# Weight conversions moved across the passes of a fast matrix product, decay rows from a scan, and a weight buffer placed elsewhere

## The chip, the cores and the metric

One core of a Trainium2 chip runs the whole kernel. The metric is the device time of one execution in microseconds (us); lower is better. The engines are named TensorE (PE; its weight loads PEld), VectorE (DVE), ScalarE (ACT), GpSimd (POOL) and SyncE (SP), whose queue issues every transfer of this kernel.

## What is computed

Three stages in a row, all in float32 precision (each float32 operand of a product is split into a high and a low part, and three products are summed).

```python
scores = scale * q @ k.T + (cum_i - cum_j)        # cum = cumsum(log(clip(f, 1e-4, 1)))
attn   = softmax(causal(scores)) ;  x = attn @ v  # 4 batches x 8 heads, 576 x 64
h = relu(x @ w_in) ** 2 ;  x = h @ w_out          # 2304 tokens, 512 -> 2048 -> 512
g = sigmoid(x @ w_gate) * (x @ w_val)             # 512 -> 1536
out = g @ w_out2                                  # 1536 -> 512
```

The weights arrive as float64. Each block of 128 x 512 is turned into float32 and split by a chain called a conversion: `conv_a` is an Abs on ScalarE (L128), `conv_b` four bit operations on VectorE (L143, L144, L147, L150; the last writes the single buffer `wf`), `conv_c` the high part on ScalarE (L164) and the low part on GpSimd (L165).

## The kernel before

**Setup and attention** (L186 to L526). `setup` (L233) loads f and takes its clipped logarithm on 32 partitions (one per head). The running sum over 576 positions is made on TensorE: the logarithms are transposed (L270), split into two parts, and multiplied with a triangle of ones (L284); the two halves of the result are copied and split (L289, L290) and written to the DRAM buffer `cum_d` (L293). `load` (L217) brings q, k and v of a pair of heads in three transfers each (L224 twice, L228). The 16 pairs of heads run through a software pipeline, whose order is a written list (`ORDER`, L499), step name and lag: TQ and TK transpose q and k (L298), qh, ql, kh, kl split them, S01 to S4 make the scores (L334, L407), R the row minima on VectorE, X the exponentials, M the normalisation on GpSimd (L422), G the transposes of the attention rows (L433), PV the product with v (L467). The decay enters the scores as one more product, with `cr`, two rows (high and low) for each of the two heads. `cr` is loaded from `cum_d` at the step kh of a pair (L384), two small transfers, and S01 of the pair reads it first.

**First up stage** (L570 on): x @ w_in, relu and square, spilled to DRAM.

**First down stage** (L705 to L766): h @ w_out, done by a scheme with seven block products in place of eight. `steps` (L605) has seven passes k_ = 0 to 6, each of 3 column groups (jj) times 4 steps (w); a step has 12 matmuls (L757). Two steps ahead, `d_split` (L613) splits a block of activations into the pair buffer `gg`, on ScalarE (L617) and VectorE (L618). VectorE also splits the weight sums `ao` (L603) in the last third of a pass and adds the finished sums (L704, L710). The order inside the stage is the program's own (`manual_schedule`). In pass 5, the block at L738 adds the conversions of the first gate and the first value block of the third stage, one phase in a step, for 12 steps.

**Second up and down stages** (L770 on). The third stage's weights are converted through `conv_q`; the scheduler may place these instructions earlier, among those of the down stage, where their buffers let it. Even blocks go to the pool `wi0`; odd ones to the pool `wi2` (L770), which before lies at the right end of SBUF, where the down stage's first weights lay.

Of the kernel before, what the change touches and what calls it, by code (L numbers as in the profile page):

```python
# [40 lines left out]
def kernel(  # L41
# [163 lines left out]
    ones_f = pts[:, 0:S]  # L205
# [2 lines left out]
    ones_u = qk[1]["kh"][:, 0:S]
    fT = qk[1]["kl"][:, 0:2 * NC * BH].rearrange("p (t c) -> p t c", t=2)
# [22 lines left out]

    def setup():  # L233
        nc.sync.dma_start(out=f_sb, in_=f.rearrange("b h s -> (b h) s"))
        for p in range(2):
# [2 lines left out]
        nc.gpsimd.memset(ones_f, 1.0)
        nc.gpsimd.affine_select(
            out=ones_f, in_=ones_f, pattern=[[1, S]], compare_op=ALU.is_ge, fill=0.0, base=0, channel_multiplier=-1  # L240
        )
        for nm_ in "qkv":
            for t in nat[nm_]:
                nc.gpsimd.memset(t[64:128, NF, :, :], 0.0)
        nc.vector.tensor_copy(ones_u, ones_f)
        for d in qk:
            for nm_ in ("cr", "eh", "el"):
                nc.gpsimd.memset(d[nm_].bitcast(F32), 0.0)
        for t in pt_t:
            nc.gpsimd.memset(t[:, 2 * POFF[NF] + S:2 * POFF[NF] + PC], 0.0)  # L250
# [20 lines left out]
        for n, w0, w1 in ((128, 0, NF * BH), (REM, NF * BH, NC * BH)):  # L271
            nc.scalar.activation(out=fT[0:n, 0, w0:w1], in_=fps[0:n, w0:w1], func=AF.Copy)
            nc.vector.tensor_tensor(
                out=fT[0:n, 1, w0:w1], in0=fps[0:n, w0:w1], in1=fT.bitcast(F32)[0:n, 0, w0:w1], op=ALU.subtract
            )
        for a, e in ((0, 256), (256, S)):
            cps = ps2()
            for c in range(NC):
                n = 128 if c < NF else REM
                s = max(a, c * 128)  # L280
                if s >= e:
                    continue
                for t in range(2):
                    nc.tensor.matmul(  # L284
                        cps[0:BH, s - a:e - a], lhsT=fT[0:n, t, c * BH:(c + 1) * BH],
                        rhs=ones_u[0:n, s - c * 128:e - c * 128],
                        start=(c == 0 and t == 0), stop=(t == 1 and c == min(NF, (e - 1) // 128)),
                    )
            nc.scalar.activation(out=cum_s[:, a:e], in_=cps[0:BH, 0:e - a], func=AF.Copy)  # L289
            nc.vector.tensor_tensor(  # L290
                out=cum_s[:, S + a:S + e], in0=cps[0:BH, 0:e - a], in1=cum_s.bitcast(F32)[:, a:e], op=ALU.subtract
            )
        nc.sync.dma_start(out=cum_d, in_=cum_s.bitcast(F32).rearrange("p (t s) -> p t s", t=2))  # L293
# [575 lines left out]
```

## Time and profile before

| | us |
|---|---|
| median of 3 runs | 1057.94 |
| the three runs | 1058.1, 1057.94, 1053.87 |
| the profiled execution | 1053.46 |
| its span, first to last instruction | 1051.6 |
| TensorE busy in the span | 1014.5 |
| VectorE / ScalarE / GpSimd busy | 561.8 / 484.6 / 254.6 |

The profile is of one execution. The attention takes the first 205 us or so, the first up stage runs to about 411, the first down stage from 411.3 to 600.2, the second up stage to about 900, and the last product to the end. TensorE's busy time counts pipelined matmuls and overlaps a little, so that where it shows a full window the engine had always something running.

### The profile page before, as it was taken

What the parts mean: (1) busy time and instruction counts of PE and PEld (TensorE: products, weight loads), DVE (VectorE), ACT (ScalarE), POOL (GpSimd) and SP (SyncE); (2) the same over time, 40 slices, a digit from 0 to 9 for tenths busy, and PEclk for the clock granted to TensorE, in tenths of its full rate; (3) what the DMA queues carried; (4) which work ended last, traced back from release to release, by engine and by line L of the source; (5) the groups of instructions that cost most, each with busy time, mean ns of one, the idle gap of its engine ahead of it and who ended that gap; (6) DMA issues with size and microseconds to landing.
All of it is one profiled execution on the core that took longest, in us unless ns stands there. A gap on an engine that the chain in (4) does not pass through costs nothing.

```text
span 1051.6 us, 16437 instructions
## 1 busy us (share of the span) xinstructions
PE 1014.5 (96%) x5915; PEld 899.2 (86%) x5915; DVE 561.8 (53%) x1131; ACT 484.6 (46%) x992; POOL 254.6 (24%) x330
## 2 busy tenths in 40 slices
PE   4999999899999999999997899999999999999998
PEld 3788788699999999999997788888888888888886
DVE  2878778555666664687689823434333421233222
ACT  3788778556666665564565422222222221222222
POOL 3766666510000121061035411111111110000000
PEclk8999999999999999999999999999999999999999
DMA  5333333057787779766665423333333311244343
GB/s 122 70 85 88 70 81 87 21 183 243 246 259 255 247 242 303 198 187 195 189 190 165 163 76 123 128 123 118 120 125 112 106 65 48 80 134 140 102 119 110
DMA packets 139217, 150.35 MB, mean 143 GB/s; under 512 B 65024, under 2 KB 110080, under 8 KB 139136
## 3 DMA queue, kind: packets, MB, share of 16 engines
q1 hardware_dynamic: 139136, 149.31, 47.4%
q8 instruction: 46, 0.75, 0.3%
q14 instruction: 35, 0.29, 0.1%
HBM read 97.21 MB, written 52.05 MB: 142 GB/s over the span
## 4 chain that ended last, share of the span: by engine, by line
PE 89%; DVE 3%; issue 3%; SPq 2%; DMA 1%; ACT 0%; POOL 0%; DVEq 0%; POOLq 0%; ACTq 0%
PE ps L549 29%; PE ps L573 18%; PE ps L812 14%; PE ps L757 13%; PE pa L334 4%; PE pa L467 4%; PE pa L433 3%; PE pa L298 2%; PE pa L407 2%; DVE gg L618 1%; SPq L224 1%; DMA cr<-cum_d 1%; SPq L228 1%; PE pa L439 1%; DVE wtmp L144 1%
## 5 line engine op out<-in xcount | busy, mean ns | idle before, releaser
L549 PE MATMUL ps<-xT,hl 128*128 128x512 f32 (+1 forms) x1440 | 300.1, 371 | 0.0
L549 PEld LDWEIGHTS ps<-xT,hl 128*128 128x128 f32 x1440 | 250.8, 188 | 49.3 <-DVE yt L710 0.3
L573 PE MATMUL ps<-xT,hl 128*128 128x384 f32 x1152 | 200.6, 335 | 1.9 <-ACT hl L164 1.1
L573 PEld LDWEIGHTS ps<-xT,hl 128*128 128x128 f32 x1152 | 199.7, 188 | 2.6 <-ACT hl L164 1.5
L757 PE MATMUL ps<-gg,ao 128*128 128x384 f32 x1008 | 178.3, 336 | 10.9 <-DVE gg L618 10.7
L757 PEld LDWEIGHTS ps<-gg,ao 128*128 128x128 f32 x1008 | 174.3, 188 | 14.8 <-DVE gg L618 14.0
L165 POOL TENSOR_TENSOR hl<-wf,hl 128x512 fp32r<-128x512 f32 x52 | 68.9, 1325 | 382.3 <-ACT hl L164 380.9
L812 PE MATMUL ps<-hl,gg 128*128 128x512 f32 x648 | 147.1, 389 | 0.0
L812 PEld LDWEIGHTS ps<-hl,gg 128*128 128x128 f32 x648 | 121.5, 188 | 25.2
L422 POOL TENSOR_TENSOR pt<-pt,sm 128x128 f32<-128x128 f32 (+2 forms) x144 | 105.8, 767 | 54.2 <-DVE sm L417 53.9
L618 DVE TENSOR_TENSOR gg<-gl,gg 128x768 fp32r<-128x768 f32 x84 | 90.5, 1081 | 40.7 <-ACT gg L617 40.5
L617 ACT ACTIVATE gg<-gl 128x768 fp32r<-128x768 f32 x84 | 71.0, 846 | 66.5 <-PE ps L757 48.0
L791 DVE TENSOR_TENSOR gg<-gi,gg 128x512 fp32r<-128x512 f32 (+1 forms) x60 | 38.4, 640 | 101.7 <-ACT gg L790 101.7
L834 DVE TENSOR_TENSOR r<-ps,r 128x512 f32<-128x512 f32 (+1 forms) x60 | 38.2, 636 | 101.8 <-PE ps L549 97.1
L641 DVE TENSOR_TENSOR gt<-gt 128x384 f32<-128x384 f32 x96 | 52.0, 584 | 70.9 <-ACT gt L675 70.9
L832 ACT ACTIVATE r<-ps 128x512 f32<-128x512 f32 (+1 forms) x60 | 32.8, 547 | 119.1 <-PE ps L549 119.1
L320 ACT ACTIVATE pt<-pt,nm 128x128 f32<-128x128 f32 (+1 forms) x144 | 82.5, 583 | 10.1 <-DVE nm L312 10.0
L790 ACT ACTIVATE gg<-gi 128x512 fp32r<-128x512 f32 (+1 forms) x60 | 35.4, 589 | 105.3 <-PE ps L812 102.3
L150 DVE SCALAR_TENSOR_TENSOR wf<-wraw,wtmp 128x512 int32<-128x512 int32 x68 | 47.8, 702 | 51.4 <-POOL hl L165 49.4
L674 ACT ACTIVATE gt<-ps 128x384 f32<-128x384 f32 x96 | 46.8, 488 | 59.4 <-PE ps L573 53.2
L312 DVE CUSTOM_DVE_ANT_0 pt<-pa,maskc 128x128 f32<-128x128 f32 (+2 forms) x144 | 67.1, 513 | 11.6 <-PE pa L334 10.8
L128 ACT ACTIVATE wtmp<-wraw 128x512 f32<-128x512 f32 x68 | 44.7, 658 | 61.7 <-DMA wraw<-in_moe_w_out_dram 41.3
(99 smaller groups left out, 1009.3 us busy)
## 6 DMA issues: line engine op xcount, KB each, us to landing
g<-gt SPq DMA_DIRECT2D x168, 192.0 KB
gl<-g SPq DMA_DIRECT2D x84, 384.0 KB
wraw<-in_moe_w_out_dram SPq DMA_DIRECT2D x28, 512.0 KB
g<-r SPq DMA_DIRECT2D x48, 256.0 KB
gi<-g SPq DMA_DIRECT2D x48, 256.0 KB
wraw<-in_moe_w_in_dram SPq DMA_DIRECT2D x16, 512.0 KB
wraw<-in_moe_w_gate_dram SPq DMA_DIRECT2D x12, 512.0 KB
wraw<-in_moe_w_val_dram SPq DMA_DIRECT2D x12, 512.0 KB
```

What stands on the lines that cost most here:

```text
L150: lambda: nc.vector.scalar_tensor_tensor(out=t.bitcast(I32), in0=lo, scalar=29, in1=xi, op0=ALU.logical_shift_right, op1=ALU.bitwise_or),
L165: nc.gpsimd.tensor_tensor(out=hl[:, 1, :], in0=t, in1=hl.bitcast(F32)[:, 0, :], op=ALU.subtract)
L312: nc.vector.tensor_tensor_reduce(out=o, in0=s, in1=mask, scale=1.0, scalar=3.0e38, op0=ALU.add, op1=ALU.min, accum_out=nm_t[p % 2][:, c:c ...
L320: nc.scalar.activation(out=x, in_=x, func=AF.Exp, bias=nm_t[p % 2][:, c:c + 1], scale=-1.0, accum_out=sm_t[p % 2][:, c:c + 1])
L422: nc.gpsimd.tensor_tensor(out=x, in0=x, in1=sm_t[p % 2][:, c:c + 1].to_broadcast([128, e - a]), op=ALU.mult)
L549: nc.tensor.matmul(h[:, 0:n], lhsT=a, rhs=x[:, b_, :], start=(c == 0 and i == 0), stop=(c == KD - 1 and i == 2))
L573: nc.tensor.matmul(h, lhsT=a, rhs=xT[c][:, b_, t0:t0 + BT], start=(c == 0 and i == 0), stop=(c == KD - 1 and i == 2))
L617: nc.scalar.activation(out=s[:, 0], in_=t, func=AF.Copy)
L618: nc.vector.tensor_tensor(out=s[:, 1], in0=t, in1=s.bitcast(F32)[:, 0], op=ALU.subtract)
L641: nc.vector.tensor_tensor(out=t, in0=a, in1=b_, op=ALU.subtract)
L757: nc.tensor.matmul(o, lhsT=ws[:, a, u, cs], rhs=s[:, b_, u, :], start=(k_ in (0, 2, 5) and w == u == x == 0), stop=(w == NW - 1 and u == 1 ...
L812: nc.tensor.matmul(o, lhsT=gg[:, a, cs], rhs=w[:, b_, :], start=(k_ == 0 and x == 0), stop=(last and x == 2))
```

## The change

1. **Setup.** The sum over positions is one VectorE instruction, `tensor_tensor_scan`, along the free axis of the 32 partitions; its high part is copied by ScalarE and its low part made by VectorE. The products, transposes and copies of L267 to L292 go, and so do the triangle of ones on GpSimd and its copy on VectorE. `cr` of the first two pairs comes straight from SBUF (`cr_load`), in the queue behind q and k of pair 1; `cum_d` is still written, and later pairs read it in a step of their own, CR, first in the list of an iteration. Memsets that only later steps need move to `setup_late`, the loads of v into the iterations, and setup is now inside the written order.
2. **Conversions.** The gate and value blocks are converted over passes 1 to 4, one phase in each column group (at w = 1), where before all was in pass 5.
3. **Odd weight buffers.** The pool `wi2` is placed from the left (low) end of SBUF, next to `wi0`.

```diff
+    def cr_load(p, source):
+        d = qk[p % 2]
+        for t in range(2):
+            nc.sync.dma_start(out=d["cr"].bitcast(F32)[t:t + 65:64, :], in_=source[2 * p:2 * p + 2, t, :])
...
+        nc.scalar.activation(out=f_sb, in_=f_sb, func=AF.Ln)
+        nc.scalar.activation(out=sm_t[0][0:BH, 0:1], in_=f_sb[:, 0:1], func=AF.Exp)
+        nc.vector.tensor_tensor_scan(out=cum_f, data0=f_sb, data1=f_sb, initial=0.0, op0=ALU.add, op1=ALU.min)
+        nc.scalar.activation(out=cum_s[:, 0:S], in_=cum_f, func=AF.Copy)
+        nc.vector.tensor_tensor(
+            out=cum_s[:, S:2 * S], in0=cum_f, in1=cum_s.bitcast(F32)[:, 0:S], op=ALU.subtract
+        )
...
+        load(1, "q")
+        cr_load(0, cum_v)
+        load(1, "k")
+        cr_load(1, cum_v)
+        nc.sync.dma_start(out=cum_d, in_=cum_v)
...
-        fps = ps2()
-        for c in range(NC):
-            n = 128 if c < NF else REM
-            nc.tensor.transpose(fps[0:n, c * BH:(c + 1) * BH], f_sb[:, c * 128:c * 128 + n], ident[0:BH, 0:BH])
...
+    def CR(p):
+        if p > 1:
+            cr_load(p, cum_d)
...
-        for h in range(2):
-            nc.sync.dma_start(out=d["cr"].bitcast(F32)[64 * h:64 * h + 2, :], in_=cum_d[2 * p + h, :, :])
...
-        S01+0 M2a+1 X4+1 M1b+1 E3+2 R0a+0 R1b+0 X3b+1 PV+2 R0b+0 R1a+0 TQ-1 M2b+1 X3a+1
+        CR-1 S01+0 M2a+1 X4+1 M1b+1 E3+2 R0a+0 R1b+0 X3b+1 PV+2 R0b+0 R1a+0 TQ-1 M2b+1 X3a+1
...
-        if k_ == 5:
-            n = NX + (3 * jj + w) // 5
-            ph = (4 * jj + w) % 6
-            n = NX + (4 * jj + w) // 6
+        if 1 <= k_ <= 4 and w == 1:
+            n, ph = divmod(3 * (k_ - 1) + jj, 6)
+            n += NX
             if ph == 0:
-                load_units(NX + 2)
                 conv_a(*units[n])
-            elif ph == 1:
                 cv[n] = conv_b(*units[n], todo=todo)
-            if todo:
-                todo.pop(0)()
+            if ph < 5:
+                if todo:
+                    todo.pop(0)()
             if ph == 5:
                 conv_c(*units[n], wi_p[0], "wi", cv.pop(n))
...
-    wi_p[1] = ctx.enter_context(tc.tile_pool(name="wi2", bufs=2, side="right", reuse_waits="tile"))
+    wi_p[1] = ctx.enter_context(tc.tile_pool(name="wi2", bufs=2, reuse_waits="tile"))
```

How the instructions moved is shown at two places. The first is SyncE's queue in the setup (cr_159 is the decay tile of pair 0, qn, kn and vn are q, k and v as loaded). Before, behind the loads of k of pair 1 and of v of pair 0:

```order
L224 DMA vn_153<-in_v_dram 128x4x64 x2
L228 DMA vn_153<-in_v_dram 64x2x64
L293 DMA cum_d<-pts 32x1152
L224 DMA vn_154<-in_v_dram 128x4x64 x2
L228 DMA vn_154<-in_v_dram 64x2x64
L224 DMA qn_148<-in_q_dram 128x4x64 x2
L228 DMA qn_148<-in_q_dram 64x2x64
L224 DMA kn_150<-in_k_dram 128x4x64 x2
L228 DMA kn_150<-in_k_dram 64x2x64
L384 DMA cr_159<-cum_d 2x576 x2
```

And now, from q of pair 1 on:

```order
L222 DMA qn_149<-in_q_dram 128x4x64 x2
L226 DMA qn_149<-in_q_dram 64x2x64
L234 DMA cr_159<-pts 2x576 x2
L222 DMA kn_151<-in_k_dram 128x4x64 x2
L226 DMA kn_151<-in_k_dram 64x2x64
L234 DMA cr_164<-pts 2x576 x2
L263 DMA cum_d<-pts 32x1152
```

The decay rows of pair 0 stand in front of k of pair 1. Six loads of three transfers each that stood ahead of them (k of pair 1, v of pairs 0 to 2, q and k of pair 2) are behind them.

The second place is VectorE in pass 5 of the first down stage, from the end of its second column group on (gg is the activation block that the next matmuls read, wtmp and wf belong to conversions, yt is a finished sum). Before:

```order
L710 TENSOR_TENSOR yt<-ps_2684,pu_4892 128x384
L710 TENSOR_TENSOR yt<-ps_2685,pu_4892 128x384
L618 TENSOR_TENSOR gg<-gl,gg 128x768
L603 TENSOR_TENSOR ao<-as,ao 128x512
L144 TENSOR_SCALAR wtmp<-wtmp 128x512
L143 TENSOR_SCALAR wtmp<-wtmp 128x512
L618 TENSOR_TENSOR gg<-gl,gg 128x768
L603 TENSOR_TENSOR ao<-as,ao 128x512
L147 SCALAR_TENSOR_TENSOR wtmp<-wraw,wtmp 128x512
L618 TENSOR_TENSOR gg<-gl,gg 128x768
L603 TENSOR_TENSOR ao<-as,ao 128x512
L150 SCALAR_TENSOR_TENSOR wf<-wraw,wtmp 128x512
```

And now, the same steps:

```order
L702 TENSOR_TENSOR yt<-ps_2657,pu_4865 128x384
L702 TENSOR_TENSOR yt<-ps_2658,pu_4865 128x384
L610 TENSOR_TENSOR gg<-gl,gg 128x768
L595 TENSOR_TENSOR ao<-as,ao 128x512
L610 TENSOR_TENSOR gg<-gl,gg 128x768
L595 TENSOR_TENSOR ao<-as,ao 128x512
L610 TENSOR_TENSOR gg<-gl,gg 128x768
L595 TENSOR_TENSOR ao<-as,ao 128x512
```

The conversions between the splits are gone here and in pass 6. The scheduler's own choices moved with the written ones: the blocks beyond the first gate and value are also begun earlier, in passes 3 to 5, and then stop. In the first column group of pass 3 four conversion instructions now stand in one step:

```order
L610 TENSOR_TENSOR gg<-gl,gg 128x768 x2
L143 TENSOR_SCALAR wtmp<-wtmp 128x512 x2
L144 TENSOR_SCALAR wtmp<-wtmp 128x512
L147 SCALAR_TENSOR_TENSOR wtmp<-wraw,wtmp 128x512
L610 TENSOR_TENSOR gg<-gl,gg 128x768 x2
L696 TENSOR_TENSOR pu_4865<-ps_2657,pu_4863 128x384
```

Three of the four belong to a block that the scheduler chose, not the written order. On VectorE the passes now hold this many conversion instructions: pass 1 three, pass 2 one, pass 3 six, pass 4 five, pass 5 three, pass 6 none; two more stand between the last finished sum and the first product of gate and value. Before, passes 1 to 4 held none and passes 5 and 6 all.

## Rows read from the trace of the kernel before

**Rows 1.** The page's chain that ended last, shares of the span by engine.

```profile
PE 89%; DVE 3%; issue 3%; SPq 2%; DMA 1%; ACT 0%; POOL 0%; DVEq 0%; POOLq 0%; ACTq 0%
```

**Rows 2.** Waits of TensorE, whole span: us in total, times, longest.

```profile
PE ps L757 <- DVE gg L618: 10.7, 10, 2.5
PE pa L334 <- DMA cr<-cum_d: 10.1, 5, 7.8
```

**Rows 3.** Timeline of the setup: start us, us, engine, line, [idle before <-releaser].

```profile
2.84 0.49 DVE L264 TENSOR_SCALAR pts<-pts 32x576 f32<-32x576 f32 x1 [2.84 <-DMA pts<-in_f_dram]
...
3.36 0.68 ACT L265 ACTIVATE pts<-pts 32x576 f32<-32x576 f32 x1 [1.27 <-DVE pts L264]
...
4.06 1.28 ACT L266 ACT_TABLE_LOAD   x1
...
4.20 0.61 SPq L228 DMA_DIRECT2D kn<-in_k_dram  x1
...
6.04 0.61 SPq L228 DMA_DIRECT2D qn<-in_q_dram  x1
...
9.30 1.23 PE L298 MATMUL pa<-ident,kn 128*128 128x128 f32 x5
...
9.54 0.65 ACT L355 ACTIVATE qh<-pa 128x576 fp32r<-128x576 f32 x1 [0.19 <-PE pa L298]
...
11.26 0.76 DVE L388 TENSOR_TENSOR kl<-pa,kh 128x576 fp32r<-128x576 f32 x1 [0.27 <-ACT kh L382]
...
18.43 0.74 SPq L384 DMA_DIRECT2D cr<-cum_d  x2
...
20.29 0.70 PE L334 MATMUL pa<-cr,one_l 64*128 64x128 f32 x2 [7.78 <-DMA cr<-cum_d]
```

**Rows 4.** Windows: stretch, its length, busy us (x) by engine, granted clock, DMA.

```profile
18.00:20.00 2.00, 0.00 (x0) 0.00 (x0) 0.00 (x0) 0.00 (x0) 0.00 (x0) 0.50 0.62 139
```

**Rows 5.** Timeline of the second pair's start, GpSimd and TensorE.

```profile
27.82 3.47 POOL L422 TENSOR_TENSOR pt<-pt,sm 128x128 f32<-128x128 f32 x6 [2.57 <-DVE sm L417]
...
28.52 0.72 PE L334 MATMUL pa<-cr,one_l 64*128 64x128 f32 x2 [0.86 <-DMA cr<-cum_d]
```

**Rows 6.** Waits of TensorE from 30 to 216 us.

```profile
PE pa L334 <- DMA cr<-cum_d: 1.4, 3, 0.9
```

**Rows 7.** Windows of passes 3 and 4, then of pass 5 and pass 6: PE, PEld, DVE, ACT, POOL.

```profile
487.80:513.20 25.40, 25.40 (x148) 25.40 (x147) 17.64 (x24) 12.71 (x17) 0.00 (x0) 1.00 0.69 192
513.20:538.60 25.40, 25.40 (x149) 25.40 (x148) 17.96 (x24) 13.93 (x21) 5.25 (x4) 1.00 0.66 186
538.60:564.00 25.40, 23.17 (x133) 22.63 (x131) 23.82 (x25) 16.69 (x25) 15.53 (x10) 1.00 0.64 187
564.00:600.00 36.00, 28.63 (x153) 26.36 (x154) 33.99 (x41) 16.32 (x25) 15.44 (x11) 1.00 0.53 168
```

**Rows 8.** Groups on VectorE, 411 to 600 us, the four conversion operations: busy us, mean ns.

```profile
L143 DVE TENSOR_SCALAR wtmp<-wtmp 128x512 f32<-128x512 f32 x7 | 7.9, 1122 | 0.0
L147 DVE SCALAR_TENSOR_TENSOR wtmp<-wraw,wtmp 128x512 int32<-128x512 int32 x7 | 6.2, 888 | 0.2
...
L144 DVE TENSOR_SCALAR wtmp<-wtmp 128x512 int32<-128x512 int32 x7 | 5.6, 796 | 0.1
L150 DVE SCALAR_TENSOR_TENSOR wf<-wraw,wtmp 128x512 int32<-128x512 int32 x5 | 4.2, 847 | 0.0
```

**Rows 9.** Timeline in pass 5: two conversions, GpSimd beside them, and TensorE's wait.

```profile
560.70 0.41 DVE L144 TENSOR_SCALAR wtmp<-wtmp 128x512 int32<-128x512 int32 x1
560.86 1.40 POOL L589 TENSOR_TENSOR as<-wf 128x512 f32<-128x512 f32 x1 [0.63 <-DVE ao L603]
561.04 1.50 DVE L143 TENSOR_SCALAR wtmp<-wtmp 128x512 f32<-128x512 f32 x1
...
564.26 2.36 PE L757 MATMUL ps<-gg,ao 128*128 128x384 f32 x12 [2.50 <-DVE gg L618]
```

**Rows 10.** The page's group of the second up stage's matmuls: busy, mean, idle before.

```profile
L549 PE MATMUL ps<-xT,hl 128*128 128x512 f32 (+1 forms) x1440 | 300.1, 371 | 0.0
```

More of the change, by code (lines that the diff above doesn't have):

```diff
@@ L204 @@
     one_l = ap_.tile([128, 256], F32R, name="one_l")
[L205 removed]
+    cum_f = pts[0:BH, 0:S]
     f_sb = pts[0:BH, S:2 * S]
     cum_s = pts[0:BH, 2 * S:4 * S].bitcast(F32R)
[L208 to L209 removed]
     ring = [0]
@@ L231, in load @@
             )
+    def cr_load(p, source):
+        d = qk[p % 2]
+        for t in range(2):
+            nc.sync.dma_start(out=d["cr"].bitcast(F32)[t:t + 65:64, :], in_=source[2 * p:2 * p + 2, t, :])
     def setup():
         nc.sync.dma_start(out=f_sb, in_=f.rearrange("b h s -> (b h) s"))
-        for p in range(2):
-            load(p, "qk")
         make_identity(nc, ident)
[L238 to L242, printed above, removed]
+        for nm_ in "qk":
             for t in nat[nm_]:
                 nc.gpsimd.memset(t[64:128, NF, :, :], 0.0)
-        nc.vector.tensor_copy(ones_u, ones_f)
+        load(0, "qk")
+        nc.vector.tensor_scalar(f_sb, f_sb, 1.0e-4, 1.0, op0=ALU.max, op1=ALU.min)
+        nc.scalar.activation(out=f_sb, in_=f_sb, func=AF.Ln)
[5 more added lines that the diff above has]
+        )
         for d in qk:
[L247 to L250, printed above, removed]
+            nc.gpsimd.memset(d["cr"].bitcast(F32), 0.0)
+        for nm_ in ("eh", "el"):
+            nc.gpsimd.memset(qk[0][nm_].bitcast(F32), 0.0)
         nc.gpsimd.memset(one_l.bitcast(F32), 0.0)
@@ L263, in setup, with setup_late @@
             )
-        nc.vector.tensor_scalar(f_sb, f_sb, 1.0e-4, 1.0, op0=ALU.max, op1=ALU.min)
-        nc.scalar.activation(out=f_sb, in_=f_sb, func=AF.Ln)
-        nc.scalar.activation(out=sm_t[0][0:BH, 0:1], in_=f_sb[:, 0:1], func=AF.Exp)
-        fps = ps2()
-        for c in range(NC):
-            n = 128 if c < NF else REM
-            nc.tensor.transpose(fps[0:n, c * BH:(c + 1) * BH], f_sb[:, c * 128:c * 128 + n], ident[0:BH, 0:BH])
[L271 to L293, printed above, removed]
+    def setup_late():
+        for nm_ in ("eh", "el"):
+            nc.gpsimd.memset(qk[1][nm_].bitcast(F32), 0.0)
+        for t in nat["v"]:
+            nc.gpsimd.memset(t[64:128, NF, :, :], 0.0)
+        for t in pt_t:
+            nc.gpsimd.memset(t[:, 2 * POFF[NF] + S:2 * POFF[NF] + PC], 0.0)
+    def CR(p):
+        if p > 1:
+            cr_load(p, cum_d)
     def transpose_in(t):
@@ L486 @@
     STEP = {
-        "TQ": TQ, "qh": qh, "ql": ql, "EH": EH, "EL": EL, "TK": TK, "kh": kh, "kl": kl,
+        "CR": CR, "TQ": TQ, "qh": qh, "ql": ql, "EH": EH, "EL": EL, "TK": TK, "kh": kh, "kl": kl,
         "S01": S01, "S2": S2, "S3": S3, "S4": S4, "PV": PV,
@@ L507 @@
         conv_q.append(("in", m, wi_p[0], "wi"))
-    setup()
     order = tc.manual_schedule()
     order.__enter__()
-    for p in range(3):
-        load(p, "v")
+    setup()
     steps = [(w[:-2], int(w[-2:])) for w in ORDER]
@@ L516 @@
     for it in range(min(lags), NP + max(lags)):
+        if it == 0:
+            setup_late()
+        if 0 <= it < 3:
+            load(it, "v")
         for nm_, lag in steps:
```

3 lines of the change are left out of this document (added).

## Prediction

> **What bounds the kernel.** I read the chain of waits first: TensorE holds 89% of it [rows 1], so a microsecond off another engine counts only where TensorE stands still for it. TensorE's waits come next. Two kinds cost about 10 us each: the first down stage's matmuls wait for the split activations of VectorE, and the attention's scores wait for the decay rows `cr` [rows 2]. The change touches both.
>
> The setup's timeline shows the second. The scores of pair 0 have nothing left but the product with `cr`, and start it at 20.29 after 7.78 us of standing still [rows 3]. The small transfer was issued only at 18.43, because it stands in SyncE's queue behind loads that nobody waits for yet. [...]
>
> The windows show the first. In passes 3 and 4 TensorE is busy for all of 25.40 us, and VectorE for 17.64 and 17.96. In pass 5 VectorE rises to 23.82, in the rest to 33.99 of 36.00, and TensorE falls to 23.17 and 28.63 [rows 7]. TensorE's idle time there is 2.23 + 7.37 = 9.6 us, nearly all of the 10.7. What was added is conversions: the four groups sum to 7.9 + 6.2 + 5.6 + 4.2 = 23.9 us [rows 8]. Without them VectorE would need 23.82 + 33.99 - 23.9 = 33.9 us of 61.4.
>
> **Term A, the setup: 10.4 us.** Now the path to the first use of `cr` is this. The clip ends at 2.84 + 0.49 = 3.33, the logarithm at 3.36 + 0.68 = 4.04 [rows 3]; both stay. The scan follows on VectorE. No row shows a scan: the nearest are the clip, 0.49 over the same 32 x 576, and the two-input subtract `kl`, 0.76 over 576 columns [rows 3]; I take 0.76 and allow double. Beside it ScalarE loads a table until 4.06 + 1.28 = 5.34 [rows 3] and does one small exponential, about 0.2, so ScalarE takes up the copy of the high part at about 5.55 at the earliest, and a scan of up to 1.5 us costs nothing. The copy I price as qh, 0.65, the subtract as kl, 0.76, with about 0.05 between steps: 6.2, then 7.0. SyncE has issued q of pair 1 by 6.04 + 0.61 = 6.65 and stands ready, so `cr` is issued at 7.0. From issue to use took 20.29 - 18.43 = 1.86 [rows 3]; used at about 8.9.
>
> [...]
>
> The other inputs of those scores are about as late. The last piece of k of pair 0 is issued at 4.20; with 2 us to land, transposes 1.23, the copy kh 0.65 and kl 0.76 [rows 3] with a little between them give 9.2 to 9.5. So the product with `cr` begins near 9.9, not at 20.29: 10.4 us. Bounds: 9.0, if a transfer from SBUF takes a microsecond longer or the scan is twice what hides; 11.9, if `cr` is ready at 9.2 and TensorE, without the long pause, also keeps the faster of its two clock levels for the next steps. What TensorE and VectorE did for the running sum falls off this path as well and is not counted again. The memsets put off (eh, el, v and pt) land on GpSimd between two pairs, where it waits 2.57 us before its next block [rows 5]: nothing. The load of k of pair 1 now stands behind a waiting `cr` and is issued at 7.7 to 9.5; its transposes come after two score groups, at about 13.5: nothing.
>
> **Term B, pair 1: 0.5 us.** Its scores waited 0.86 for `cr` [rows 5]; now `cr` of pair 1 is in place by 12. But GpSimd's first block of normalisations ends at 31.29 (27.82 + 3.47), and the transposes that read most of it come right there, so part of the wait turns into a wait for GpSimd. Bounds 0 and 0.86; I take the middle.
>
> **Term C, later pairs: 1.2 us.** Three waits of 1.4 us in sum [rows 6]. The step CR issues the rows at the start of the iteration before, ahead of v, q and k, so 1.86 us of travel has a whole iteration as cover. It waits for the last scores that read the buffer, which end the iteration before that; the loads behind it in the queue wait for later steps of TensorE anyway. Bounds 0.7 and 1.4.
>
> **Term D, the down stage: 9.0 us.** Passes 5 and 6 lose almost all conversions and should look like passes 3 and 4: TensorE without idle time, 9.6 us gained. What they cost in their new place: at the means of the groups, which include being held up, pass 3 gets two each of L143, L144 and L147, 2 x (1.12 + 0.80 + 0.89) = 5.6 us, and pass 4 gets 1.12 + 0.80 + 0.89 + 2 x 0.85 = 4.5 [rows 8]. The room is 25.40 - 17.64 = 7.8 and 25.40 - 17.96 = 7.4 [rows 7]. So they fit even at these prices; passes 1, 2 and 5 get fewer. A split is made two steps of 25.40 / 12 = 2.1 us ahead, so VectorE may fall behind by part of that before TensorE sees it. The four conversions in one step of pass 3 cost between 4 x 0.41 = 1.6 us [rows 9] and 3.9 at the means; I leave 0.6 us for such places. Bounds 7.0 and 9.6. The two conversions left over at the stage's end stand ahead of the first product of gate and value on VectorE, and two high parts ahead of the first sigmoid on ScalarE: some 5 us of delay there, but TensorE has eight banks, each filled in 300.1 / 120 = 2.5 us, before it needs one back, and the second up stage showed no idle time before its matmuls [rows 10]; I price it at nothing, and if that cover fails it costs up to 5 us.
>
> **The sum.** 10.4 + 0.5 + 1.2 + 9.0 = 21.1 us. From the profiled execution, 1053.46, that gives 1032.4; from the median, 1057.94, it gives 1036.8. Two of three runs lie near 1058 and one at 1053.87, with the profile; nothing in it says why. I take 1034.
>
> **Rivals.** *The wait moves to passes 3 and 4.* A conversion takes 0.41 alone and 1.50 beside a GpSimd instruction that starts meanwhile [rows 9]. In passes 1 to 4 fifteen conversion instructions and two low parts (L165) now stand beside GpSimd's sums. If each is held up by a third of a microsecond and all of it reaches TensorE, 5 us come back: 1039. For: the collisions are in the rows. Against: the means above contain them and still fit, and pass 3 has no GpSimd work at all [rows 7].
> [...]
>
> *The decay rows come late.* If the path to `cr` has 5 us that I don't see (transfers between places in SBUF behind the loads' packets), A is halved: 1039.
>
> *The gain of D is given back.* If the second up stage waits for its second pair of weights, since their buffer comes free only after the last sum of pass 6, up to 9 us come back: 1043. Against: the weights are needed a whole column of weights later, 300.1 / 12 = 25 us [rows 10].
>
> *Slower.* One mechanism could do it: the scan. It is serial, and no row prices a serial instruction. B, C and D bring 10.7 us, so to lose 5.3 in all `cr` must be used 16 us later than before, at 36.3, which needs a scan of about 29 us: 50 ns an element, where the subtract takes 0.76 us / 576 = 1.3 ns. Then the time is 1059 or more.
>
> That the change doesn't do what it says can be left out for the order: the rows of the new order show the conversions gone from passes 5 and 6 and the queue changed.
>
> **Chances.** Forecast 0.76, wait moved 0.10, rows late 0.06, given back 0.04, slower 0.02, and 0.02 for no difference. A measurement of this kernel can tell about 0.5%, 5.3 us, from no change; all named cases but the last two are faster by more. So faster 0.95, same 0.03, slower 0.02. The forecast's own range is 1029.5 (1053.46 less the upper bounds, 23.8) to 1041 (1057.94 less the lower, 16.7). I give 1028 to 1042, which takes in the first two rivals and most of the third.
>
> **What would show it.** Right: the first product with `cr` near 10 us; a scan under 1.5 us; no wait of TensorE for `cr` anywhere; the down stage some 9 us shorter, with VectorE below 24 us in each pass. Wrong: waits for gg in passes 3 and 4; a wait of the scores for `cr` above 1 us or for kl; idle time ahead of L549's matmuls (L541 now); a scan longer than 2 us.

## The result and the profile after

| | before | after |
|---|---|---|
| median, us | 1057.7 | 1029.47 |
| single runs, us | 1058.1, 1057.94, 1053.87, 1057.45 | 1029.5, 1029.43, 1030.48, 1028.18 |
| profiled execution, us | 1053.46 | 1029.5 |
| its span, us | 1051.6 | 1027.5 |

The ratio is 0.974, with a 95% interval of 0.9715 to 0.9765. The time predicted was 1034, the range 1028 to 1042. Between the two profiled executions the gain is 24.0 us; between the medians it is 28.2. In the experiments below the kernel before was run 34 times more, with medians of 1053.45 to 1054.88, so the profile with its 1053.46 stands for it better than the first runs near 1058; why those were slower stayed open. Against those medians 1029.47 is a ratio of 0.976 to 0.977.

The first matmuls of the stages, read from TensorE's timeline, tell where the time went. The changed kernel's lines are some 8 to 10 lower: L749 is the L757 of before, L541 the L549, L565 the L573, L326 the L334, L610 the L618.

| stage, us | before | after | gain |
|---|---|---|---|
| start to first matmul of the first up stage | 208.98 | 193.70 | 15.28 |
| first up stage | 202.33 | 203.93 | -1.60 |
| first down stage | 189.05 | 182.77 | 6.28 |
| second up stage | 299.98 | 296.16 | 3.82 |
| last product, to the end of the span | 151.26 | 150.94 | 0.32 |

The setup of the changed kernel in the timeline, with the same columns as [rows 3]:

```profile
2.63 0.83 DVE L243 TENSOR_SCALAR pts<-pts 32x576 f32<-32x576 f32 x1 [2.63 <-DMA pts<-in_f_dram]
...
4.20 1.28 ACT L245 ACT_TABLE_LOAD   x1
4.22 1.35 DVE L246 TENSOR_TENSOR_SCAN pts<-pts 32x576 f32<-32x576 f32 x1 [0.75 <-ACT pts L244]
...
5.61 0.67 ACT L247 ACTIVATE pts<-pts 32x576 fp32r<-32x576 f32 x1
6.31 0.74 DVE L248 TENSOR_TENSOR pts<-pts 32x576 fp32r<-32x576 f32 x1 [0.75 <-ACT pts L247]
6.72 1.24 SPq L234 DMA_DIRECT2D cr<-pts  x2
...
9.21 0.47 PE L326 MATMUL pa<-kl,qh 64*128 64x128 f32 x2 [0.32 <-DVE kl L378]
...
9.69 0.42 PE L326 MATMUL pa<-cr,one_l 64*128 64x128 f32 x2
```

The scan ends at 5.57, almost with the table load that hides it (5.48), and the first product with `cr` starts at 9.69 without a wait, where it started at 20.29 after 7.78 us of one [rows 3]. The last wait ahead of it is now 0.32 us for `kl`.

TensorE's two longest waits after (us in total, times, longest); `cr` is gone from the whole list, and of the 10.7 us for `gg` [rows 2] 4.5 are left:

```profile
PE pa L290 <- POOL one_l L257: 4.6, 1, 4.6
PE ps L749 <- DVE gg L610: 4.5, 7, 1.6
```

The windows of passes 2 to 6 of the first down stage after, with the columns of [rows 7]:

```profile
448.40:473.80 25.40, 24.41 (x140) 23.87 (x139) 20.67 (x23) 13.58 (x20) 8.49 (x6) 1.00 0.72 204
473.80:499.20 25.40, 25.15 (x143) 24.33 (x142) 21.64 (x30) 13.61 (x19) 2.72 (x2) 1.00 0.67 189
499.20:524.60 25.40, 25.40 (x148) 25.40 (x147) 18.75 (x26) 13.59 (x20) 5.00 (x4) 1.00 0.68 206
524.60:550.00 25.40, 23.44 (x133) 22.58 (x132) 19.03 (x26) 14.44 (x23) 13.13 (x9) 1.00 0.64 193
550.00:580.40 30.40, 30.17 (x172) 29.30 (x170) 22.13 (x23) 14.20 (x22) 15.06 (x10) 1.00 0.50 142
```

VectorE is below 23 us in every one of them, against 33.99 of 36.00 in pass 6 before. Yet pass 5 still loses 1.96 us of TensorE (25.40 - 23.44) and pass 2 loses 0.99. The timeline shows the place of pass 5, on VectorE, GpSimd and TensorE:

```profile
525.69 1.30 POOL L165 TENSOR_TENSOR hl<-wf,hl 128x512 fp32r<-128x512 f32 x1
...
527.02 0.69 DVE L150 SCALAR_TENSOR_TENSOR wf<-wraw,wtmp 128x512 int32<-128x512 int32 x1 [2.17 <-POOL hl L165]
...
527.63 0.95 DVE L610 TENSOR_TENSOR gg<-gl,gg 128x768 fp32r<-128x768 f32 x1
...
528.64 2.54 PE L749 MATMUL ps<-gg,ao 128*128 128x384 f32 x13 [1.58 <-DVE gg L610]
```

VectorE stands still for 2.17 us ahead of a conversion that writes `wf`, since GpSimd has not finished reading the block before from that single buffer. The split `gg` is queued behind, and TensorE waits 1.58 us for it.

The second up stage had no wait before [rows 10] and has none now, but its 1440 matmuls take 296.3 us in place of 300.1:

```profile
L541 PE MATMUL ps<-xT,hl 128*128 128x512 f32 (+1 forms) x1440 | 296.3, 368 | 0.0
```

### The profile page after: what moved, and what is told of

Same layout as the page of the kernel before. It is cut to its first block, busy times and chain, and to the rows that moved or that the text cites. A ratio compares the mean times of both kernels' runs of the same rounds, so it can differ in the third digit from the quotient of the medians.

```text
span 1027.5 us, 16430 instructions
## 1 busy us (share of the span) xinstructions
PE 1005.9 (98%) x5896; PEld 896.8 (87%) x5896; DVE 556.9 (54%) x1128; ACT 482.8 (47%) x989; POOL 255.4 (25%) x328
## 4 chain that ended last, share of the span: by engine, by line
PE 87%; DVE 4%; DMA 3%; issue 2%; ACT 2%; POOL 1%; SPq 0%; ACTq 0%; POOLq 0%; DVEq 0%
PE ps L541 29%; PE ps L565 19%; PE ps L804 14%; PE ps L749 9%; PE pa L326 4%; PE pa L457 4%; PE pa L423 3%; DMA gl<-g 2%; DVE gg L610 2%; PE pa L290 2%; PE pa L397 2%; ACT gg L609 1%; DVE ao L595 1%; PE pa L429 1%; DMA wraw<-in_moe_w_out_dram 0%
## 5 line engine op out<-in xcount | busy, mean ns | idle before, releaser
L541 PE MATMUL ps<-xT,hl 128*128 128x512 f32 (+1 forms) x1440 | 296.3, 368 | 0.0
L541 PEld LDWEIGHTS ps<-xT,hl 128*128 128x128 f32 x1440 | 250.8, 189 | 45.5 <-DVE yt L702 0.3
L565 PE MATMUL ps<-xT,hl 128*128 128x384 f32 x1152 | 202.4, 337 | 1.7 <-ACT hl L164 1.0
L565 PEld LDWEIGHTS ps<-xT,hl 128*128 128x128 f32 x1152 | 201.4, 189 | 2.5 <-ACT hl L164 1.3
L749 PE MATMUL ps<-gg,ao 128*128 128x384 f32 x1008 | 178.4, 336 | 4.5 <-DVE gg L610 4.5
L749 PEld LDWEIGHTS ps<-gg,ao 128*128 128x128 f32 x1008 | 174.3, 188 | 8.4 <-DVE gg L610 8.1
L165 POOL TENSOR_TENSOR hl<-wf,hl 128x512 fp32r<-128x512 f32 x52 | 67.8, 1304 | 369.5 <-ACT hl L164 369.4
L610 DVE TENSOR_TENSOR gg<-gl,gg 128x768 fp32r<-128x768 f32 x84 | 92.1, 1101 | 40.0 <-ACT gg L609 39.6
L150 DVE SCALAR_TENSOR_TENSOR wf<-wraw,wtmp 128x512 int32<-128x512 int32 x68 | 47.8, 703 | 59.6 <-POOL hl L165 57.5
```

Of the source, the lines that this page charges most:

```text
L150: lambda: nc.vector.scalar_tensor_tensor(out=t.bitcast(I32), in0=lo, scalar=29, in1=xi, op0=ALU.logical_shift_right, op1=ALU.bitwise_or),
L165: nc.gpsimd.tensor_tensor(out=hl[:, 1, :], in0=t, in1=hl.bitcast(F32)[:, 0, :], op=ALU.subtract)
L541: nc.tensor.matmul(h[:, 0:n], lhsT=a, rhs=x[:, b_, :], start=(c == 0 and i == 0), stop=(c == KD - 1 and i == 2))
L565: nc.tensor.matmul(h, lhsT=a, rhs=xT[c][:, b_, t0:t0 + BT], start=(c == 0 and i == 0), stop=(c == KD - 1 and i == 2))
L610: nc.vector.tensor_tensor(out=s[:, 1], in0=t, in1=s.bitcast(F32)[:, 0], op=ALU.subtract)
L749: nc.tensor.matmul(o, lhsT=ws[:, a, u, cs], rhs=s[:, b_, u, :], start=(k_ in (0, 2, 5) and w == u == x == 0), stop=(w == NW - 1 and u == 1 ...
```

## The experiments

The theory after the result: each part of the change gave several microseconds, but the sum agreed partly by luck. The decay rows' new place in the queue gave three times what the waits in the trace named; the down stage gained less than forecast, and the low weight buffers did something there and in the second up stage that the forecast had at nothing. The rivals: the spreading alone carries the down stage, and the second up stage gained from the conversions, not from an address.

### One part at a time (e1 to e4)

e1, e2 and e3 are the kernel before with part 1, 2 or 3 alone; e4 is the changed kernel without part 3. The lines of e2 and e3 against the kernel before, and of e4 against the changed one (e1 takes all of part 1 over):

```diff
e2 (and the lines of part 2 around these, as in the change):
-        if k_ == 5:
...
-            n = NX + (4 * jj + w) // 6
+        if 1 <= k_ <= 4 and w == 1:
+            n, ph = divmod(3 * (k_ - 1) + jj, 6)
...
e3:
-    wi_p[1] = ctx.enter_context(tc.tile_pool(name="wi2", bufs=2, side="right", reuse_waits="tile"))
+    wi_p[1] = ctx.enter_context(tc.tile_pool(name="wi2", bufs=2, reuse_waits="tile"))
e4:
-    wi_p[1] = ctx.enter_context(tc.tile_pool(name="wi2", bufs=2, reuse_waits="tile"))
+    wi_p[1] = ctx.enter_context(tc.tile_pool(name="wi2", bufs=2, side="right", reuse_waits="tile"))
```

> The kernel before with part 1 of the change alone: setup with the scan, decay rows issued early (step CR at the start of an iteration); conversions and odd weight buffers as before. Theory: the first product with cr starts near 9.7 us as in the changed kernel, the attention runs at its steady 10.98 us a pair from the start, so the first down matmul of the first up stage stands 15.3 us earlier than 208.98; the first up stage gives 1.6 us back in a clock dip; down stage and second up stage are those of before (189.1 and 300.0 us). Profiled run 1053.46 - 13.7 = 1039.8. Rival: the 4.2 us beyond the setup come from elsewhere in the change; then only 10.9 to 12 us are gained by 209 us, and the time is 1041.5 to 1042.6, or 1043 to 1044 with the clock dip.

> The kernel before with part 2 alone: the gate and value conversions spread over passes 1 to 4 of the first down stage, odd weight buffers high as before. Theory: the high buffers are free earlier, so the scheduler fills passes 5 and 6 with conversions again, and the stage gains 2 to 5 us of its 189.1, less than the 6.3 us of the whole change; the second up stage stays at 300.0 us with odd blocks of 25.34 us. Profiled run 1048.5 to 1051.5. Rival: the spreading alone carries the whole gain of the stage: 6.3 us, 1047.2. A second rival, that the second up stage's gain of 3.8 us comes with the spreading too: 1043.4.

> The kernel before with part 3 alone: the odd weight buffers of the second up stage low in SBUF. Theory (the address of the buffer): all blocks of the second up stage take 24.66 us, where odd ones took 25.34, and the stage 296.2 instead of 300.0 us, with nothing else done: 1049.6 if the down stage keeps its 189.1 us, up to 2 us less or more if the scheduler places conversions otherwise. Rival (the gain of the second up stage comes from the conversions' new place): the stage stays at 300.0 us and the time at 1053.5.

> The changed kernel with part 3 undone: the odd weight buffers high in SBUF again. Theory (the address): the second up stage goes back to 300.0 us, odd blocks to 25.34 us; the down stage, with conversions placed again in passes 5 and 6, is 0 to 3 us longer than 182.8: 1033.3 to 1036.3 against 1029.5. Rival (address without effect, the gain belongs to the conversions): the second up stage stays at 296.2 us and the time at 1029.5 to 1032.5.

| kernel | median, us | profiled | to first up | up | down | second up |
|---|---|---|---|---|---|---|
| before | 1054.52 here | 1053.46 | 208.98 | 202.33 | 189.05 | 299.98 |
| e1, part 1 | 1040.07 | 1039.95 | 195.04 | 202.34 | 189.46 | 300.00 |
| e2, part 2 | 1052.24 | 1052.91 | 209.26 | 203.90 | 186.54 | 299.99 |
| e3, part 3 | 1045.08 | 1045.08 | 209.39 | 202.36 | 183.83 | 296.14 |
| e4, parts 1 and 2 | 1038.26 | 1039.69 | 194.81 | 203.93 | 187.87 | 300.00 |
| after | 1029.47 | 1029.5 | 193.70 | 203.93 | 182.77 | 296.16 |

The ratios to the kernel before are 0.9865 (0.985 to 0.9879) for e1, 0.998 (0.9968 to 0.9991) for e2, 0.9913 (0.9898 to 0.9928) for e3 and 0.9849 (0.9832 to 0.9866) for e4.

Part 1 holds 13.9 of the 15.3 us ahead of the first up stage; the nine kernels with the changed attention begin that stage between 193.54 and 195.04 us, so the rest is within what one and the same code shows. e1's time agrees by two misses that cancel: it gained 1.4 us less there than expected, and the clock dip of 1.6 us that its expectation took off did not come. e2 missed its time since its first up stage lost the 1.6 us, and e4 since its down stage grew by 5.1 and not by up to 3. Part 2, the spreading, shortens the down stage by only 2.5 us alone and by 1.6 beside part 1 (e4 against e1). Part 3 alone shortens it by 5.2 us, and gives the whole 3.8 us of the second up stage: the theory on the buffers' place holds there, in e3 and in e4, and e3's time is lower than it said by the 5.2 us of the down stage, of which it had left most out.

How far single profiles carry here is told by five kernels whose instructions stand in one and the same order on TensorE, VectorE, ScalarE and GpSimd in the down stage. The changed kernel, e5, e6, e9 and e11 took 182.77, 179.59, 183.56, 180.38 and 182.12 us in it, with a wait in pass 5 of 0.68 to 1.58 us. Part 2's 1.6 to 2.5 us are inside that spread of 4.0. Part 3's 5 us are above it, and come out with and without part 2. Part of it is how far VectorE runs ahead. The conversion that runs beside a GpSimd instruction in pass 2 (L150, 1.50 us in all three, against 0.69 in pass 5 of the changed kernel) starts 58.1 us after the stage's first matmul in the changed kernel, where TensorE waits 0.99 us behind it, and 56.6 and 57.6 in e5 and e9, where TensorE doesn't wait. Why the lead differs is not shown.

TensorE's waits in passes 5 and 6, one row each for before, e2, e3, e4 and after:

```profile
PE ps L757 <- DVE gg L618: 9.6, 8, 2.5
```

```profile
PE ps L757 <- DVE gg L618: 5.5, 5, 1.8
```

```profile
PE ps L757 <- DVE gg L618: 4.6, 4, 2.5
```

```profile
PE ps L749 <- DVE gg L610: 4.3, 5, 1.8
```

```profile
PE ps L749 <- DVE gg L610: 2.1, 3, 1.6
```

By these rows part 2 alone takes off 4.1 us and part 3 alone 5.0; e2 gives some of it back in passes 2 and 3, with waits of 0.71 and 0.21 us.

How part 3 does this is read from the buffers' addresses and the order, and only in part shown. The high place (bytes 221152 to 229344 of a partition) lies inside the first weights `wf1`, which the last weight sums leave free well before the stage ends, so the scheduler brings the third stage's next blocks to VectorE and GpSimd in passes 5 and 6; the high part (L164) of the next gate block runs in pass 6. The low place (112768 to 120960) overlaps the first of the three partial sums `pu`, and the same L164 stands behind the last finished sums of the stage, with the other conversions queued up behind it. Before, then after:

```profile
577.07 0.64 ACT L164 ACTIVATE hl<-wf 128x512 fp32r<-128x512 f32 x1 [2.21 <-DVE wf L150]
```

```profile
581.69 0.62 ACT L164 ACTIVATE hl<-wf 128x512 fp32r<-128x512 f32 x1
```

The sums of passes 5 and 6 no longer read that first partial sum, only the other two, so what holds L164 to the end there is not shown. That the buffer beneath decides, and not the side, is borne out by e6 below. Its odd buffers lie high again, but the first of them over a buffer of the split weight sums `ao`; VectorE's order in the down stage is that of the changed kernel, and L164 waits for the stage's last matmuls:

```profile
580.77 0.63 ACT L164 ACTIVATE hl<-wf 128x512 fp32r<-128x512 f32 x1 [4.81 <-PE ps L749]
```

### The written order to the end, and the conversions in pass 3 (e7, e8, e12)

```diff
e7, against the changed kernel (in e7, e8 and e12):
-    order.__exit__(None, None, None)
     dn.close()
...
+    order.__exit__(None, None, None)
     conv_some(len(conv_q))
e8, in addition:
-        if 1 <= k_ <= 4 and w == 1:
-            n, ph = divmod(3 * (k_ - 1) + jj, 6)
...
+        if k_ == 3:
...
+            ph = (4 * jj + w) % 6
+            n = NX + (4 * jj + w) // 6
...
e12, in addition to e8: the pool wi2 with side="right"
```

> The changed kernel with the written order kept up to the last conversions of the second up stage, so that the scheduler cannot pull third-stage conversions of the weights into passes 5 and 6 of the down stage. Theory (what is left of TensorE's waits in the down stage comes from conversions that the scheduler placed there, above all the one that held VectorE for 2.17 us behind GpSimd at 527): waits of 1.58, 0.37 and 0.18 us go, the stage takes 180.7 us instead of 182.8, the time is 1027 to 1028. Rival (the last conversions, now in the written order, come too late for the second up stage): TensorE waits ahead of an odd block, 1029.5 to 1034.

> The run above with both blocks' written conversions in pass 3 instead of spread over passes 1 to 4. Theory (a conversion costs TensorE time only where GpSimd works beside it, and pass 3 has no work of GpSimd): the waits of 0.99 and 0.21 us in passes 2 and 3 go as well, the stage takes 179.5 us, the time is 1026 to 1027. Rival (what matters is VectorE's load in a pass; pass 3 then holds 17.6 + about 10 us of conversions, over its 25.4): waits for gg of 2 to 4 us in pass 3, and 1029 to 1032.

> The run e8 (written order up to the end of the second up stage, conversions in pass 3) with the odd weight buffers high again, so that the scheduler cannot bring conversions back and only the address is changed. Theory (part 3 works in two ways, by keeping the scheduler's conversions out of passes 5 and 6, some 5 us, and by the address, 3.8 us): the down stage stays at 177.6 us, the second up stage goes from 296.2 to 300.0, the time is 1029 us. Rival (the address is the whole of part 3): the down stage is longer by 5 us as well, 1034.

| kernel | median (runs), us | ratio to before | down | second up |
|---|---|---|---|---|
| e7 | 1028.06 (1026.15 to 1029.08) | 0.9744 (0.9728 to 0.9759) | 179.64 | 296.09 |
| e8 | 1025.23 (1023.89 to 1026.41) | 0.9715 (0.9699 to 0.9731) | 177.60 | 296.00 |
| e12 | 1028.09 (1026.88 to 1029.32) | 0.9747 (0.9731 to 0.9763) | 177.91 | 299.85 |

e7's theory holds in the trace: no wait above 0.14 us is left in passes 5 and 6. Its time does not settle it: 179.64 is inside the 179.59 to 183.56 of the unchanged order, and its runs overlap with the changed kernel's (1028.18 to 1030.48). e8 and e12, at 177.60 and 177.91, are below all of those. Their theories hold, with e8's gain 1.9 us larger than forecast; its rival was not put to the test, since pass 3 held 21.06 us of VectorE work and not more than 25.4. In e8 the four operations of a conversion on VectorE, in pass 3, take no longer than 0.69 us each; GpSimd's one instruction in that pass is the low part of this block, and it comes after them:

```profile
479.55 0.42 DVE L143 TENSOR_SCALAR wtmp<-wtmp 128x512 f32<-128x512 f32 x1
481.63 0.42 DVE L144 TENSOR_SCALAR wtmp<-wtmp 128x512 int32<-128x512 int32 x1
483.71 0.68 DVE L147 SCALAR_TENSOR_TENSOR wtmp<-wraw,wtmp 128x512 int32<-128x512 int32 x1
486.11 0.69 DVE L150 SCALAR_TENSOR_TENSOR wf<-wraw,wtmp 128x512 int32<-128x512 int32 x1
487.56 1.55 POOL L165 TENSOR_TENSOR hl<-wf,hl 128x512 fp32r<-128x512 f32 x1 [12.91 <-ACT hl L164]
```

In the changed kernel the same L150 in pass 2 starts beside GpSimd's split of a finished sum (L688) and takes 1.50, and the splits behind it 2.0 each beside GpSimd's weight sums (L581), which is the 0.99 us that TensorE loses there:

```profile
455.33 1.37 POOL L688 TENSOR_TENSOR xT<-yt,xT 128x384 fp32r<-128x384 f32 x1 [2.78 <-ACT xT L687]
455.75 1.50 DVE L150 SCALAR_TENSOR_TENSOR wf<-wraw,wtmp 128x512 int32<-128x512 int32 x1
...
456.66 3.70 POOL L581 TENSOR_TENSOR as<-wf 128x512 f32<-128x512 f32 x2
...
457.17 4.00 DVE L610 TENSOR_TENSOR gg<-gl,gg 128x768 fp32r<-128x768 f32 x2
...
459.26 1.51 PE L749 MATMUL ps<-gg,ao 128*128 128x384 f32 x7 [0.99 <-DVE gg L610]
```

So L150 took 0.69 us where GpSimd stood still (for 12.91 us ahead of its L165 in e8) and 1.50 beside GpSimd's split; the split `gg` took 0.95 in pass 5 (527.63, above), when GpSimd's L165 had ended, and 2.0 beside the weight sums. Why VectorE's instructions are longer beside GpSimd's is not shown. What is left of TensorE's waits for `gg` in e8 stands in the first steps of the stage and is 1.1 us; the stage's 177.60 is seven passes of 25.4 within 0.2. e12 takes part 3's two effects apart: with the written order, the high buffers cost 0.3 us in the down stage (177.91) and 3.85 us in the second up stage. e8 beats the changed kernel by 4.2 us of median. Their runs don't overlap, and the profiles' down stages differ by 5.2.

### Where the decay rows are issued (e5, e9)

```diff
e5, against the changed kernel (the list ORDER; CR-1 goes from first to behind kh-1):
-        CR-1 S01+0 M2a+1 X4+1 M1b+1 E3+2 R0a+0 R1b+0 X3b+1 PV+2 R0b+0 R1a+0 TQ-1 M2b+1 X3a+1
+        S01+0 M2a+1 X4+1 M1b+1 E3+2 R0a+0 R1b+0 X3b+1 PV+2 R0b+0 R1a+0 TQ-1 M2b+1 X3a+1
...
e9, in addition:
-            cr_load(p, cum_d)
+            d = qk[p % 2]
+            for h in range(2):
+                nc.sync.dma_start(out=d["cr"].bitcast(F32)[64 * h:64 * h + 2, :], in_=cum_d[2 * p + h, :, :])
```

The place behind kh is the middle of the list, as in the kernel before; the expectation for e5 calls it the end.

> The changed kernel with one step moved: the decay rows of pairs 2 and on (step CR) are issued behind kh, at the end of an iteration's list, where the kernel before issued them, instead of at its start. Theory (the issue's place carries the 4.2 us that the attention gained beyond the setup): short waits for cr come back in pairs 2 to 8, the first matmul of the first up stage stands 3 to 4.5 us later than 193.7, and the time is 1032.5 to 1034. Rival (the place is worth only the 1.4 us of waits that the trace of before names): 195.1, and 1031.

> The changed kernel with the decay rows of pairs 2 and on issued as the kernel before did it, in place and in form: behind kh, one transfer for each head (the run e5 had moved the place but kept the new form, one transfer for each of the two parts of both heads, so that each head waits for both). Theory (place and form together made the 4.2 us): the first matmul of the first up stage stands 4 to 5 us later than 193.7, the time is 1033 to 1034.5. Rival (the place alone makes the 16 us that e5 lost): 209 us, and 1041 to 1042.

e5 took 1042.27 us (1041.16 to 1044.91), ratio 0.9884 (0.9867 to 0.9902), with the first up stage at 209.66; e9 took 1033.64 (1031.34 to 1037.91), ratio 0.9813 (0.978 to 0.9847), with it at 202.07. So the place matters by more than either side of e5's expectation had it, and so does the form: 16.0 us in the new form (209.66 - 193.70), 8.4 in the old, of which one wait of 2.66 stands at pair 2. Of the 8.4, 3.8 come ahead of the first product with v and 4.5 behind it, where the change had gained 4.2. e9's theory is right in the median (+4.2) and too low by half in this stretch; the time agrees by luck, since e9's first up and down stages were 1.6 and 2.4 us shorter than the changed kernel's with the same instructions in the same order. The timeline of one pair shows the lead of the transfer, and how a late one costs time that no view of waits names. Before, the issue and the end of the group of scores that needs the rows:

```profile
80.70 0.76 SPq L384 DMA_DIRECT2D cr<-cum_d  x2
...
81.31 0.50 PE L334 MATMUL pa<-kh,ql 64*128 64x512 f32 x2
...
82.50 0.29 PE L334 MATMUL pa<-kh,qh 64*128 64x128 f32 x2
82.64 0.41 PE L334 MATMUL pa<-cr,one_l 64*128 64x128 f32 x2
82.75 0.47 PE L334 MATMUL pa<-kh,ql 64*128 64x256 f32 x2
...
83.50 0.76 PE L467 MATMUL pa<-pts,vn 128*64 128x256 f32 x6
```

After:

```profile
80.88 1.06 SPq L234 DMA_DIRECT2D cr<-cum_d  x2
...
90.62 0.50 PE L326 MATMUL pa<-kh,ql 64*128 64x512 f32 x2
...
91.80 0.29 PE L326 MATMUL pa<-kh,qh 64*128 64x128 f32 x2
91.92 0.29 PE L326 MATMUL pa<-cr,one_l 64*128 64x128 f32 x2
92.03 0.35 PE L326 MATMUL pa<-kh,ql 64*128 64x256 f32 x2
...
92.66 2.92 PE L457 MATMUL pa<-pts,vn 128*64 128x256 f32 x28
```

In e5, where the same lateness is large enough to get its bracket:

```profile
78.32 0.33 PE L326 MATMUL pa<-cr,one_l 64*128 64x128 f32 x2 [0.46 <-DMA cr<-cum_d]
```

The transfer now has 11.0 us from its issue to this product (80.88 to 91.92), where it had 1.9 (80.70 to 82.64). From the first score of the group (81.31 before, 90.62 after) to the product with v are 2.19 us before and 2.04 after. Before, the matmuls with `cr` and behind it are stretched (0.41 for 0.29, 0.47 for 0.35), and neither has a bracket with a wait, since the one ahead, by its modelled end, still runs when the late one starts. The time from one pair's product with v to the next (the last one, 8.8 in both, left out) was 11.02 to 12.29 us for the first ten and 10.98 or 10.99 for the other three before; it is 10.98 or 10.99 for all of them now. The differences sum to 4.2 us.

### Where the odd weights lie (e6, e10, e11)

```diff
e6: wi2 with bufs=10, side="right"
e10: the same, with the pool gp opened ahead of wi2 and wo behind it
e11: wi2 with bufs=10, on the left
```

> The changed kernel with ten instead of two odd weight buffers, at the high end: the odd blocks of the second up stage read their weights from five places, block 1 from byte 188384 of a partition on, block 3 from 196576, block 5 from 204768, block 7 from 212960, block 9 from 221152 (the place of the kernel before), block 11 from 188384 again. Theory (an address near the end of SBUF is slow): block 9 takes 25.34 us, blocks 1 and 11 take 24.66, with the step somewhere between; the stage gains 2 to 3.5 of the 3.8 us. Rival (all of the high side is slow against the low one): all odd blocks take 25.34 us. Second rival (what matters is that two buffers are used in turn, or what lies beside them): none takes 25.34. The scheduler is free to place conversions earlier, so the down stage may be up to 8 us longer than 182.8.

> The changed kernel with ten odd weight buffers between bytes 163808 and 204768 of a partition, and the last product's split activations gg from 217056 on. Gate and value of the odd blocks read from: block 1 163808 and 200672, block 3 196576 and 192480, block 5 188384 and 167904, block 7 172000 and 176096, block 9 180192 and 184288, block 11 as block 1. In the run before all places from 188384 on gave 396 ns for a matmul of 512 columns, the low ones 389. Theory (weights read from above some address between 120960 and 188384 cost 7 ns more a matmul, and the last product, whose weights lay below 180192 and took 389 ns, shows that this address is above about 176000): block 7 takes 389, block 3 396, blocks 1, 5 and 11 some 392 to 393, block 9 between; and the last product rises from 389 to 396 ns a matmul, about 4 us. Rival (the whole upper side is slow where the moving operand lies low, and the last product is different since its moving operand lies high): all odd blocks 396 ns, the last product 389 as before.

> The changed kernel with ten odd weight buffers on the low side, between bytes 112768 and 153728 of a partition. Gate and value of the odd blocks read from: block 1 112768 and 149632, block 3 145536 and 141440, block 5 137344 and 116864, block 7 120960 and 125056, block 9 129152 and 133248, block 11 as block 1. All places from 163808 on gave 396 ns a matmul of 512 columns, those up to 120960 gave 389. Theory (the step stands at an address, and it is the address that counts): block 7 takes 389, block 3 396 or 389 according to the side of the step, blocks 1 and 5 between if the step lies below 137344. Rival (what counts is that the buffers lie on the right-hand side of the allocation, not an address): all blocks 389.

The single runs took 1033.45, 1032.09 and 1030.12 us, the second up stages 299.98, 299.98 and 296.14. One block of weights per row: the matmuls of 512 columns (count, busy us, mean ns) in 16 us out of an even and an odd block of the kernel before (weights at 104576 and 108672, then at 221152 and 225248), then of block 7 in e10 (weights at 172000 and 176096) and of block 3 in e11 (145536 and 141440):

```profile
L549 PE MATMUL ps<-xT,hl 128*128 128x512 f32 x73 | 16.7, 389 | 0.0
L549 PE MATMUL ps<-xT,hl 128*128 128x512 f32 x70 | 16.6, 396 | 0.0
```

```profile
L541 PE MATMUL ps<-xT,hl 128*128 128x512 f32 x70 | 16.6, 396 | 0.0
```

```profile
L541 PE MATMUL ps<-xT,hl 128*128 128x512 f32 x72 | 16.5, 389 | 0.0
```

Every odd block of e6 and e10 shows 396, every block of e11 and every even block 389. (In e6 the places turned out to be used in another order than the expectation gives; all lie at 188384 or above.) The first rival of e6 and the rival of e10 won: there is no step from 163808 up. The last product speaks against a plain rule of addresses: with its weights at 217056 and above in e10, it stays at

```profile
L804 PE MATMUL ps<-hl,gg 128*128 128x512 f32 x648 | 147.1, 389 | 0.0
```

and in e6, with weights between 126944 and 139232, it does too. In e11 the rival won as well, as far as it goes: weights up to 153728 on the left cost nothing. Whether the step lies between 153728 and 163808, or the side of the allocation decides by some other way, stays open, and so does the cause.

## Why the prediction was right, and where its steps were not

**Term A: right.** 10.4 us forecast, 10.60 measured (20.29 to 9.69). The clip took 0.83 and not 0.49; ScalarE's table load and small exponential, which end at 5.70, hid the scan, which ended at 5.57, as worked out. The scan took 1.35 us, inside the doubled bound, against 0.74 of the subtract of the same size. The two clock levels that the upper bound of 11.9 speaks of are in the trace: the granted clock before is 1.00 up to 13.75 us, 0.50 from 14.00, in the pause, to 24.00, with the first scores after it, and 1.00 from 24.25 to 30; now it is 1.00 from the start to 30 us.

**Term B: right in size.** The first product with v starts at 26.76 and not 37.81: 11.05 us, so 0.45 beside A's 10.60; 0.5 forecast. The 0.45 is the sum of all that changed in between. As forecast, part of the wait for `cr` came back as another one, but the one that the list shows is 0.66 us for `ql` from VectorE (L351), not one for GpSimd.

**Term C: mis-sized.** 1.2 us forecast, with an upper bound of 1.4 from the sum of the waits [rows 6]; measured are 4.2 (from the first product with v to the first up stage 171.17 us before, 166.94 after). The step that failed is taking the view of waits as the bound: a late matmul whose forerunner, by its modelled end, still runs is in no such list. The period of a pair would have shown it. e1 puts the gain in part 1, and e9, with the old place and form of the issue, loses it again (171.47).

**Term D: mis-sized, and without its main cause.** 9.0 forecast, bounds 7.0 to 9.6; measured 6.3, below the lower bound. The step that failed is "I leave 0.6 us for such places". What stands against the 9.6 us is 3.3: the collision in pass 2 (0.99), the stall for `wf` in pass 5 (1.58), and three of 0.18 to 0.37. The second is no collision; it is a conversion of a later block that the scheduler still put there, and e7 takes it away. The size is that of one profile: e5 and e9, with the same order, took 179.59 and 180.38 us, 9.5 and 8.7 below the kernel before, with no wait in pass 2 and 0.68 and 0.73 in pass 5. The collision in pass 2 is there too, but VectorE is further ahead and TensorE doesn't feel it. The working took the conversions' leaving passes 5 and 6 from the new order and gave part 3 no term. e2 and e4 show that the spreading alone gains 1.6 to 2.5; it is part 3 that keeps the others out. The count of conversions was right, and the cause was half seen.

**The second up stage: missed.** It was priced at nothing, with up to 5 us to lose, and gained 3.8. It had no waits [rows 10], but no waits is not the same as full speed: the odd blocks ran at 396 ns a matmul. The mean of 371 ns in that row mixes them, and matmuls of 256 columns besides.

**The first up stage: not looked at.** It lost 1.6 us. The granted clock in it, before and then after (length, TensorE's busy time, clock, DMA):

```profile
214.98:217.98 3.00, 2.27 (x14) 1.00 0.81 195
217.98:220.98 3.00, 3.00 (x19) 1.00 0.86 284
```

```profile
199.70:202.70 3.00, 2.26 (x9) 0.70 0.77 197
202.70:205.70 3.00, 3.00 (x15) 0.74 0.62 225
```

The same six microseconds get a mean of 0.70 and 0.74, and 24 matmuls where 33 stood. In quarters of a microsecond the clock after is 0.50 from 201.00 to 204.25 and 1.00 on both sides, with one mixed quarter (0.75 and 0.93) at each end; before it is 1.00 throughout. Worked out from these quarters, that is 1.7 us of the full clock, beside the 1.6 lost. Of the 14 profiled kernels six have the stage at 202.33 to 202.39 and eight at 203.85 to 203.94; in these two windows, counted from the stage's start, the six show 1.00 and the eight 0.64 to 0.80. So the clock is the loss. Part 2 doesn't decide it: e5, e6 and e9 hold the change's part 2 and are among the six. What does decide it is open.

**The sum.** 21.1 forecast; measured 15.28 - 1.60 + 6.28 + 3.82 + 0.32 = 24.1. C and the second up stage gave 6.8 us more, D and the first up stage took 4.3 back. The time was inside the range, but the errors partly cancel. The 24.0 us between the profiles are even more than the sum of the forecast's upper bounds, 23.8 (which puts the lower end at 1029.7, not 1029.5); that the stated range began at 1028 took it in.

**The rivals.** The wait did move to pass 2 and 3, by 1.2 us and not 5. The decay rows were not late, nothing was given back in the second up stage, and the scan did not grow.

## What to carry to other kernels

Before a list of waits is taken as the bound of a gain, compare the period of the loop with that of a pair that has no wait: 1.4 us in the list were 4.2 in the periods. Where a stage alternates between two buffers, look at the time of every second block even when nothing waits. Where a written order ends before the next stage, ask what a scheduler can put into the place that comes free: here most of the down stage's gain came from a buffer whose place held it back, and a written order to the end, with the conversions beside no GpSimd work, gave 5.2 us more in the profiles, and 1.7 us at the least against the shortest stage with the unchanged order (177.91 against 179.59).
